# Top-k attention with a maxout MLP: batch 1 in token order too, new ordering offsets, two spans for the last batch

## The chip, the cores and the metric

One Trainium2 chip, one core. The metric is the device time of one execution in microseconds. PE is the matmul engine (PEld its weight loads), DVE, ACT and POOL the vector, scalar and GpSimd engines, SP the engine that issues the transfers.

## The reference

```python
batch, n_heads, seq, head_dim = (8, 8, 576, 64)
top_k = 32
scores = scale * np.matmul(q, k.transpose(0, 1, 3, 2))
kth = np.partition(scores, -top_k, axis=-1)[..., -top_k:-top_k + 1]
mask = scores >= kth
scores = np.where(mask, scores, -1000000000.0)
scores = scores - np.max(scores, axis=-1, keepdims=True)
attn = np.exp(scores)
attn = attn / (np.sum(attn, axis=-1, keepdims=True) + 1e-09)
attn_out = np.matmul(attn, v)
x = attn_out.transpose(0, 2, 1, 3).reshape(4608, 512)
h = np.maximum(np.maximum(x @ w1, x @ w2), x @ w3)   # 512 x 768 weights
out = h @ w_out                                      # 768 x 512
```

All is float32. So each query row keeps its 32 largest scores of 576, and the attention output goes through an MLP whose hidden layer is the maximum of three products.

## The kernel before, in words

**Attention.** A unit (`units`, L872) is a batch, one head pair and two tiles of 128 query tokens, called (0, 1) and (2, 3); the last 64 tokens of two head pairs make a narrow unit of one tile. Ten units make a batch, eight wide and two narrow. For a unit, PE makes the scores (`qk`, L514), ACT moves them to SBUF (`evac`, L523), DVE takes the eight largest of each of 8 groups (`sweep`, L532) and works a pivot out of them, ACT and POOL take the scores on one side of the pivot (L571, L576), DVE finds the threshold among them (L580) and masks the scores (`mask`, L619), ACT exponentiates (`expo`, L628), PE transposes (L679), ACT moves the result (L687), PE multiplies with v (`values`, L704), and DVE, ACT and POOL write the result x as a high and a low float16 part (L721, L724, L728). Before a head pair is used its q and k are loaded by SP (`load_qk`), transposed by PE (L454, L465), scaled by ACT (L460, L469), rounded by ACT (L470) and their rest taken by POOL (L474): one preparation (`prep`, `prepare`). Only two head pairs' preparations are held at a time, six tiles of v, and x for two batches. The scale of v is common to the batch, so that the first values of a batch need all four of its v tiles.

**MLP.** `mlp` (L735) works on spans of tokens of a batch: 0 to 256 as soon as all heads have written these tokens, then 256 to 576. For a span and each of 6 blocks of the hidden layer, three products of 12 matmuls each (`layer`, L760; float16 high and low parts), whose maximum is taken by ACT and DVE (L767, L769) and split by ACT and POOL (L772, L775). Then the output matmuls for each tile of 128 tokens (`layer2`, L820), a scaled copy by ACT (L825) and a store by SP. For the last batch the second span is cut in two, 256 to 512 and 512 to 576 (L1056). A span has 6 x 3 x 12 = 216 matmuls of L760, whatever its width.

**Order.** Nothing of the order on an engine is left to the compiler. Each operation is a `Piece` with an engine, a planned cost, the pieces that it needs, and the buffers that it takes (`Ring`). `in_order` (L65) plans the run, piece by piece, and issues each engine's instructions in that order. A piece's rank is the place of its unit, counted in tiles, plus an offset of its kind from `OFFSETS` (L38; the key `s00` is the first sweep, `m0` the first mask, `Pl` to `Pz` the preparation, `D` and `C` the weights). For each engine the pieces are tried in order of rank, those no more than `LEAD` above the lowest rank that is left; the first that can start within `PATIENCE` (ns) of the earliest is taken. The MLP's pieces stand in a queue of their own (`fill`): on PE one of them goes ahead when it can start more than `AHEAD_OF_FILL` ns before the attention piece; on the other engines they are tried first. DVE pieces marked `alone`, the masks among them, are planned apart from POOL's work. The weights are loaded, decoded on DVE and cut into parts in the first part of the run.

**Batch 0** (`SPLIT`, L133; `batch`, L859) is worked in token order: first the units (0, 1) of all head pairs, in the order 2, 3, 0, 1, then all the rest, head pairs 0 and 1 and then 2 and 3. As only two preparations are held, those of head pairs 2 and 3 are made twice. The other batches go by head pairs: (0, 1) and (2, 3) of pair 0, (0, 1) of pair 1, the narrow unit, (2, 3) of pair 1, and then the same with pairs 2 and 3. In the last batch the second group is sorted so that (0, 1) of both come first and the narrow unit last. The program has 34 preparations.

After the last batch a flag is formed from the numbers that `review` keeps; a second path, for inputs where the threshold was not found, is not taken here.

Of the kernel before, what the change touches and what calls it, by code (L numbers as in the profile page):

```python
# [28 lines left out]
GAP = 100.0  # L29
NEAR = 110.0  # L30
SWITCH = 95.0
AHEAD_OF_FILL = 3
WINDOW = 150
LEAD = 43.3
SLACK = 2000.0
LOCK_A = -150.0
LOCK_B = -100.0
OFFSETS = {'C0': -8.46, 'C1': -18.47, 'C2': 3.93, 'C3': 15.97, 'D0': -3.87, 'D1': -3.6, 'D2': -21.98, 'D3': 12.25, 'E00': 3.88, 'E01': 0.84, 'E02': -2.21, 'E10': -0.98, 'E11': -2.42, 'E12': -13.91, 'N': 0.27, 'Pa': -3.56, 'Pl': -8.36, 'Pp': 14.6, 'Pz': 7.25, 'R': 10.23, 'S': -1.09, 'T00': -15.17, 'T01': -13.99, 'T02': 4.17, 'T10': -11.04, 'T11': -8.12, 'T12': 22.63, 'U': -1.67, 'U0': 2.18, 'V': -13.7, 'V0': -0.21, 'Y': 0.84, 'Z': -6.48, 'd0': 7.84, 'd1': -2.02, 'e00': -1.82, 'e01': -1.45, 'e10': -1.05, 'e11': 1.55, 'g0': 1.61, 'g1': -2.4, 'g2': 1.3, 'g3': -10.18, 'h0': 2.46, 'h1': -2.33, 'h2': 1.34, 'k0': 0.45, 'k1': -2.6, 'k2': 2.19, 'k3': -8.03, 'm0': -18.11, 'm1': -7.69, 'm2': -3.59, 'm3': -1.01, 'p1': 3.73, 'p2': 4.11, 'p3': -13.92, 'p4': -15.96, 'p5': 2.73, 'q0': -0.76, 'q1': -0.22, 'r0': 1.77, 'r1': -17.21, 's00': 5.74, 's01': 5.23, 's10': 5.37, 's11': 6.45, 'v': 13.6, 'w0': 9.7, 'w1': 11.03, 'w2': 0.57, 'w3': 18.45, 'x0': 3.87, 'x1': 2.76, 'x2': 8.01, 'x3': 5.15, 'y': -13.4, 'z0': 3.01, 'z1': 4.39}  # L38
AHEAD = 4
LATE = {'PE': 102.0, 'DVE': 60.0, 'ACT': 95.0, 'POOL': 10.0, 'SP': 2000.0}  # L40

# [88 lines left out]


WS_ACT = range(12)
SPLIT = (0,)  # L133
FIRST = ((0, 1),)
NSM = 2
PATIENCE = {'PE': 2.0, 'DVE': 159.0, 'ACT': 47.0, 'POOL': 7.0, 'SP': 0.0}


@with_exitstack
def kernel(ctx, tc, q, k, v, moe_w1, moe_w2, moe_w3, moe_w_out, out):  # L140
    nc = tc.nc
    B, H, S, D = q.shape
    P = 128
    C = S // 64
    NP = H // 2
    NU = S // P
# [167 lines left out]
    def piece(engine, cost, run, needs=(), rank=(0.0, None), takes=(), mode=None, alone=False):  # L314
        x = Piece(engine, cost, run, needs, rank, [(rings[r], rel) for r, rel in takes], mode, alone)
        pieces.append(x)
        return x
# [102 lines left out]
    def load_qk(b, hp):  # L420
        tiles = []
        for src, nm in ((q, "qt"), (k, "kt")):
            t = io.tile([P, NU, 2, D], F32, name=nm, bufs=1)
            for h in range(2):
                nc.sync.dma_start(t[:, :, h, :], main_rows(src, b, 2 * hp + h))
            tiles.append(t)
        t = io.tile([P, 2, D], F32, name="last", bufs=1)
        for w, src in enumerate((k, q)):
            nc.sync.dma_start(t[64 * w:64 * w + 64], src[at.get(b, b), 2 * hp:2 * hp + 2, MAIN:S].rearrange("h p d -> p h d"))
        tiles.append(t)  # L430
        qk_of[b, hp] = tiles
# [303 lines left out]
    def mlp(b, first, spans, tiles, alone, needs, rank):  # L735
# [4 lines left out]
        products, every, done = [], [], {}  # L740

        def add(engine, cost, run, needs=(), takes=(), mode=None):
            x = Piece(engine, cost, run, needs, rank, [(rings[r], rel) for r, rel in takes], mode)
            every.append(x)
            if engine == "PE":
                if products:
                    x.needs.append(products[-1])
                products.append(x)
            return x

        def layer(i, f, kcs, c0, c1, box):
            if first and not H:
                H.extend(wk.tile([P, FC, HW], F16, name=nm, bufs=1) for nm in ("hh", "hl"))
            xh, xl = x_of[b]
            if kcs[0] == 0:
                box["ps", i] = ps_m.tile([P, 512], F32, name="m")
            for kc in kcs:
                high, low = halves(i, kc, f * P, P)
                for k, (a, bb) in enumerate(((high, xh), (low, xh), (high, xl))):
                    nc.tensor.matmul(box["ps", i][:, :c1 - c0], a, bb[:, kc, c0:c1], start=(kc == 0 and k == 0),  # L760
                                     stop=(kc == KC - 1 and k == 2))
# [15 lines left out]
        for c0, c1 in spans:  # L777
            w = c1 - c0
            base = c0 if c0 < MAIN else c0 - 2 * P
            cs = slice(off + c0 - base, off + c1 - base)  # L780
            for f in range(FC):
                box, prev, before = {}, None, []
                for i in range(3):
                    rel = []
                    for kcs in ((0, 1), (2, 3)):
                        x = add("PE", 6 * max(0.423 * w, 64.0), lambda i=i, f=f, kcs=kcs, c0=c0, c1=c1, box=box: layer(i, f, kcs, c0, c1, box),
                                [*needs, *(lows[i * KC + kc, f * P // CUT * CUT] for kc in kcs if lows)],
                                [("m", rel)] if kcs[0] == 0 else [])
                    now = []
                    y = add("DVE" if i else "ACT", 117 + 1.047 * w if i else 152 + 0.844 * w, lambda i=i, w=w, box=box: largest(i, w, box),  # L790
                            [x, *prev] if i else [x], [("h1", now)])
                    rel.append(y)
                    if i:
                        before.append(y)
                    before, prev = now, [y]
                y = add("ACT", 87 + 0.85 * w, lambda f=f, cs=cs, w=w, box=box: high_h(f, cs, w, box), prev)
                z = add("POOL", 150 + 1.906 * w, lambda f=f, cs=cs, w=w, box=box: low_h(f, cs, w, box), [y])
                before.extend([y, z])
                done.setdefault(f, []).append(z)
        last = products[-1]  # L800
# [36 lines left out]
        for u in tiles:  # L837
# [3 lines left out]
            n = P if u < NU or both else 64  # L841
            at0 = off + u * P - base
            cs = slice(at0, at0 + n)
            box, rel, used = {}, [], []
            for f in range(FC):
                x = add("PE", 3 * 215.0, lambda f=f, cs=cs, n=n, box=box: layer2(f, cs, n, box),
                        [*done[f], *(z for k, z in lows.items() if k[0] == 3 * KC + f)], [("m", rel)] if f == 0 else [])
            y = add("ACT", 585, lambda n=n, both=both, box=box: scaled_out(n, both, box), [x, so_at[b]], [("ob", used)])
# [24 lines left out]
    n = len(units)  # L873
    place_of = [sum(len(x[2]) for x in units[:i]) for i in range(n)]

    preps, starts, prep_of = [], [], []
# [7 lines left out]
    def attention(n):  # L884

        b, hps, us = units[n]
# [51 lines left out]
        for g in gs:  # L938
# [7 lines left out]
            for i in range(3):  # L946
                rel = []
# [8 lines left out]
        rel, takes = [], []  # L956
# [39 lines left out]
    load_last, users = [], [[] for _ in preps]  # L996

    def prepare(pi):
        b, hp = preps[pi]
        rank = starts[pi]  # L1000
        load = piece("SP", 4000, lambda: load_qk(b, hp), list(load_last), (rank, "Pl"))
        box = {}
        load_last.clear()
        done, last = [], list(load_bits)
        load_bits.clear()
        for k in range(3):
            def products(k=k):
                if k == 0:
                    box["turns"] = prep(b, hp)
                box["turns"][k][0]()  # L1010
            rel = []
            x = piece("PE", 109 if k == 0 else 436, products, [load, *done[-1:]], (rank, "Pp"), [("tr", rel)])
            y = piece("ACT", 169 if k == 0 else 1211, lambda k=k: box["turns"][k][1](), [x, *last, *done[-1:]], (rank, "Pa"))
            rel.append(y)
            load_last.append(x)
            if pi >= 2:
                users[pi - 2].append(x)
            done.append(y)
            if k:
                z = piece("POOL", 1380, lambda k=k: box["turns"][k][2](), [y], (rank, "Pz"))  # L1020
                done.append(z)
                load_bits.append(z)
        prepared[pi] = done
# [29 lines left out]
    parts_of = {b: [(True, [(0, 2 * P)], (0, 1)), (False, [(2 * P, S)], range(2, NU + 1))] for b in range(B)}  # L1053
    if len(FIRST) > 1:
        parts_of[0] = [(True, [(0, P)], (0,)), (False, [(P, 2 * P)], (1,)), (False, [(2 * P, S)], range(2, NU + 1))]
    parts_of[B - 1] = [(True, [(0, 2 * P)], (0, 1)), (False, [(2 * P, 4 * P)], (2, 3)), (False, [(4 * P, S)], (NU,))]  # L1056
    for b in range(B):
        for first, spans, tiles in parts_of[b]:
            us = [u for u in range(NU + 1) if any(c0 < u * P + 64 <= c1 or c0 < (u + 1) * P <= c1 for c0, c1 in spans)]
            needs = [z for (hp, u), z in z_of[b].items() if u in us]  # L1060
            products, every, last = mlp(b, first, spans, tiles, False, needs, (0.0, None))
# [89 lines left out]
```

## Time and profile before

| what | us |
|---|---|
| median of 3 runs | 1276.28 (1276.07 to 1277.53) |
| the profiled execution | 1279.52 |
| its span, first to last instruction | 1277.8 |
| PE, DVE, ACT, POOL busy | 1165.9, 1157.3, 1118.2, 684.9 |

The span lies inside the execution's own time; 1.7 us are around it. Busy time is the time in which at least one instruction of the engine ran. Matmuls are pipelined and their ends are modelled, so a PE that is busy all the time isn't thereby at its peak. PEclk is the mean share of full speed that TensorE's clock was granted in a stretch.

### The profile page before, as it was taken

The numbers are of one execution on the slowest core, as the hardware profiler recorded it, in microseconds if no ns is written. First come the engines' busy times: TensorE is split into PE (matmuls) and PEld (weight loads), VectorE is DVE, ScalarE is ACT, GpSimd is POOL, SyncE is SP. The second block draws the span as 40 slices with busy tenths as digits, with TensorE's granted clock in tenths as the row PEclk, the third lists the DMA queues.
The fourth block names the chain that finished last, engine by engine and source line by source line (L and its number), as shares of the span: only waits on it lengthen the run. The fifth ranks groups of instructions, "written<-read, shape, count | busy, mean of one in ns | idle before, by whom it ended". The sixth has DMA issues, their size and how long they took to land.

```text
span 1277.8 us, 30699 instructions
## 1 busy us (share of the span) xinstructions
PE 1165.9 (91%) x9949; PEld 855.3 (67%) x9949; DVE 1157.3 (91%) x5736; ACT 1118.2 (88%) x2912; POOL 684.9 (54%) x625
## 2 busy tenths in 40 slices
PE   4337897999799999999999999999999999999997
PEld 3224574766487766867686766867787777867775
DVE  6999999999999999999999999999999999999221
ACT  5699989999999999999999999999999999998321
POOL 4538477664565565655465565555556555545110
PEclk9667899899799999999999999999999999999999
DMA  7341110211011012110111011010111100000000
GB/s 223 129 117 45 51 38 17 49 38 46 20 39 41 25 29 54 30 36 25 51 38 37 20 37 47 20 53 22 46 30 46 30 21 26 20 18 2 17 18 28
DMA packets 107018, 53.58 MB, mean 42 GB/s; under 512 B 91745, under 2 KB 99937, under 8 KB 106849
## 3 DMA queue, kind: packets, MB, share of 16 engines
q1 hardware_dynamic: 106848, 51.54, 14.7%
q8 instruction: 80, 1.31, 0.4%
q14 instruction: 90, 0.73, 0.2%
HBM read 42.07 MB, written 9.44 MB: 40 GB/s over the span
## 4 chain that ended last, share of the span: by engine, by line
PE 33%; DVE 26%; ACT 20%; POOL 4%; issue 2%; SPq 0%; DMA 0%; ACTq 0%; DVEq 0%; POOLq 0%
PE m L760 16%; DVE L L532 6%; DVE ssb L619 6%; DVE Q L580 4%; ACT w L571 4%; PE m L820 4%; ACT pm L628 4%; PE tr L704 4%; ACT pT L687 4%; PE tr L679 4%; POOL w L576 3%; PE s L514 3%; ACT ssb L523 3%; DVE h L769 2%; DVE nR L556 1%
## 5 line engine op out<-in xcount | busy, mean ns | idle before, releaser
L576 POOL TENSOR_TENSOR w<-ssb,w 128x576 f32<-128x576 f32 x288 | 413.6, 1454 | 135.2 <-ACT w L571 134.3
L760 PE MATMUL m<-xh,wall 128*128 128x256 f16 (+2 forms) x2448 | 436.9, 279 | 1.3 <-DVE h L769 0.6
L760 PEld LDWEIGHTS <-wall 128*128 128x128 f16 x3672 | 343.8, 98 | 79.7 <-issue 7.4
L760 PE MATMUL m<-xl,wall 128*128 128x256 f16 (+2 forms) x1224 | 335.2, 279 | 0.0
L532 DVE MAX8 L<-ssb 128x8 f32<-128x72 f32 x2304 | 329.7, 219 | 2.2 <-ACT ssb L523 2.2
L619 DVE SCALAR_TENSOR_TENSOR ssb<-ssb,kth 128x576 f32<-128x576 f32 x288 | 240.8, 864 | 2.3
L628 ACT ACTIVATE pm<-ssb,nb 128x576 f32<-128x576 f32 x288 | 225.5, 785 | 18.5 <-DVE ssb L619 18.3
L571 ACT ACTIVATE w<-ssb,Q 128x576 f32<-128x576 f32 x288 | 226.1, 786 | 6.8 <-DVE Q L563 6.8
L687 ACT COPY pT<-tr 128x512 f32<-128x512 f32 (+1 forms) x432 | 217.8, 520 | 11.3 <-PE tr L676 7.9
L580 DVE MAX8 Q<-w 128x8 f32<-128x576 f32 x288 | 213.9, 750 | 9.7 <-POOL w L576 8.3
L679 PE MATMUL tr<-ident,pm 128*128 128x128 f32 x1152 | 183.3, 285 | 28.4 <-ACT pm L628 13.2
L514 PE MATMUL s<-kT,qT 64*128 64x288 f32 x1920 | 179.8, 322 | 23.0 <-ACT ssb L523 14.7
L523 ACT COPY ssb<-s 128x576 f32<-128x576 f32 x288 | 185.0, 646 | 4.2 <-PE s L514 3.8
L679 PEld LDWEIGHTS tr<-ident,pm 128*128 128x128 f32 x1152 | 130.8, 143 | 80.2 <-ACT pm L628 27.3
L704 PE MATMUL tr<-pT,vt 128*64 128x256 f32 (+1 forms) x1920 | 180.9, 340 | 2.3 <-ACT pT L687 2.1
L514 PEld LDWEIGHTS s<-kT,qT 64*128 64x128 f32 x1920 | 140.6, 195 | 62.0 <-issue 23.8
L775 POOL TENSOR_TENSOR hl<-h,hh 128x256 f16<-128x256 f32 (+2 forms) x102 | 78.3, 768 | 180.2 <-ACT hh L772 171.1
L769 DVE SCALAR_TENSOR_TENSOR h<-m,rises,h 128x256 f32<-128x256 f32 (+2 forms) x204 | 100.4, 492 | 60.1 <-PE m L760 55.9
L704 PEld LDWEIGHTS tr<-pT,vt 128*64 128x64 f32 x1920 | 109.5, 141 | 60.9 <-issue 15.8
L820 PE MATMUL m<-wall,hh 128*128 128x512 f16 x432 | 128.9, 379 | 3.6 <-POOL wall L305 1.9
L728 POOL TENSOR_TENSOR xl<-xs,xh 128x256 f16<-128x256 f32 (+1 forms) x80 | 52.4, 655 | 126.6 <-ACT xh L724 126.6
L474 POOL TENSOR_TENSOR kT<-raws,kT 128x576 fp32r<-128x576 f32 x34 | 49.7, 1462 | 86.2 <-ACT kT L470 83.8
(109 smaller groups left out, 1468.2 us busy)
## 6 DMA issues: line engine op xcount, KB each, us to landing
wall<-in_moe_w_dram SPq DMA_DIRECT2D x12, 768.0 KB, 5.9
qt<-in_q_dram SPq DMA_DIRECT2D x68, 128.0 KB, 2.9
kt<-in_k_dram SPq DMA_DIRECT2D x68, 128.0 KB, 3.0
out_dram<-ob SPq DMA_DIRECT2D x32, 256.0 KB, 2.3
vt<-in_v_dram SPq DMA_DIRECT2D x32, 128.0 KB, 2.1
vt<-in_v_dram SPq DMA_DIRECT2D x32, 64.0 KB, 2.2
vt<-in_v_dram SPq DMA_DIRECT2D x96, 16.0 KB, 2.0
vt<-in_v_dram SPq DMA_DIRECT2D x32, 48.0 KB, 2.2
```

The costliest lines, as they stand in the source:

```text
L514: nc.tensor.matmul(s[:, h, :HALF], qT[sl, qa, c0:c0 + P], kT[sl, ka, i * HALF:(i + 1) * HALF], start=(n_ == 0), stop=(n_ == len(runs) - 1))
L523: nc.scalar.copy(d["both", g][:, :, i * HALF:(i + 1) * HALF], d["s"].pop((g, i))[:, :, :HALF])
L532: nc.vector.max(d["L"][:, t, k, :], d["ssb"][t][:, k * GW:(k + 1) * GW])
L571: nc.scalar.activation(d["w"][t], d["ssb"][t], AF.Sign, bias=d["Q"][:, t, 0:1], scale=-1.0, accum_out=d["cnt"][:, t:t + 1])
L576: nc.gpsimd.tensor_tensor(d["w"][t], d["ssb"][t], d["w"][t], ALU.mult)
L580: nc.vector.max(d["Q"][:, t, 1:NW], d["w"].pop(t))
L619: nc.vector.scalar_tensor_tensor(ss, ss, d["kth"][:, t:t + 1], ss, ALU.is_lt, ALU.subtract, accum_out=d["lost"][:, t:t + 1])
L628: nc.scalar.activation(d["pm", t // 2][:, t % 2], d["ssb"][t], AF.Exp, bias=d["nb"][:, t:t + 1], scale=-1.0 / SHRINK, accum_out=d["sums"][ ...
L679: nc.tensor.transpose(pt[:, j * P:(j + 1) * P], pm[:, i, 64 * i + j * P:64 * i + (j + 1) * P], ident)
L687: nc.scalar.copy(pT[:, 512 * i:512 * i + m] if i < 2 else pT[:, 8 * P:10 * P], pt[:, :m])
L704: nc.tensor.matmul(to, vt[:, block if i < 4 else 8 + h, :], keys, start=(i == 0), stop=(i == 4))
L760: nc.tensor.matmul(box["ps", i][:, :c1 - c0], a, bb[:, kc, c0:c1], start=(kc == 0 and k == 0), stop=(kc == KC - 1 and k == 2))
```

## The change

Batch 1 joins batch 0 in `SPLIT`, so its units go in token order too; its head pairs 2 and 3 are then prepared twice, and the program has 36 preparations. The line that cut the last batch's MLP in three spans goes, so that it has two like the others. The pieces of batch 0's units and preparations get keys of their own, with an underscore in front, in `OFFSETS`; all offsets have new values. `LEAD`, `PATIENCE` and `AHEAD_OF_FILL` have new values, and the planned cost of an MLP matmul is changed: 0.9 ns more for wide ones, and a lower floor for narrow ones. No instruction of a unit or of the MLP changes in kind.

```diff
-AHEAD_OF_FILL = 3
+AHEAD_OF_FILL = 21
-LEAD = 43.3
+LEAD = 73.4
-OFFSETS = {'C0': -8.46, 'C1': -18.47, 'C2': 3.93, 'C3': 15.97, 'D0': -3.87, 'D1': -3.6, 'D2': -21.98,
...
+OFFSETS = {'C0': -24.16, 'C1': -8.19, 'C2': 8.62, 'C3': 19.5, 'D0': -5.71, 'D1': -5.65, 'D2': -49.21,
...
+ '_Pa': -2.68, '_Pl': -11.11, '_Pp': -3.76, '_Pz': -17.42, '_T00': -32.25, '_T01': -13.55, '_T02': 7.86,
...
-SPLIT = (0,)
+SPLIT = (0, 1)
-PATIENCE = {'PE': 2.0, 'DVE': 159.0, 'ACT': 47.0, 'POOL': 7.0, 'SP': 0.0}
+PATIENCE = {'PE': 27.0, 'DVE': 197.0, 'ACT': 65.0, 'POOL': 109.0, 'SP': 0.0}
...
-                        x = add("PE", 6 * max(0.423 * w, 64.0), lambda ...
+                        x = add("PE", 6 * max(0.423 * w + 0.9, 29.0), lambda ...
...
-        p = lambda key, *a, **kw: ... rank=(place_of[n], key ...
+        p = lambda key, *a, **kw: ... rank=(place_of[n], ("_" if b == 0 else "") + (key ...
...
-        rank = starts[pi]
-        load = piece("SP", 4000, lambda: load_qk(b, hp), list(load_last), (rank, "Pl"))
+        rank, first_ = starts[pi], "" if b else "_"
+        load = piece("SP", 4000, lambda: load_qk(b, hp), list(load_last), (rank, first_ + "Pl"))
...
     parts_of = {b: [(True, [(0, 2 * P)], (0, 1)), (False, [(2 * P, S)], range(2, NU + 1))] for b in range(B)}
...
-    parts_of[B - 1] = [(True, [(0, 2 * P)], (0, 1)), (False, [(2 * P, 4 * P)], (2, 3)), (False, [(4 * P, S)], (NU,))]
```

## Rows read from the trace of the kernel before

**Rows 1.** The page's first part: busy time, share of the span, instructions.

```profile
PE 1165.9 (91%) x9949; PEld 855.3 (67%) x9949; DVE 1157.3 (91%) x5736; ACT 1118.2 (88%) x2912; POOL 684.9 (54%) x625
```

**Rows 2.** Stretches by stage: length, busy of each engine, PEclk, DMA share, GB/s.

```profile
0.00:148.00 148.00, 75.80 (x412) 49.50 (x413) 133.79 (x520) 115.44 (x284) 78.40 (x89) 0.75 0.40 122
148.00:240.00 92.00, 79.17 (x706) 58.91 (x704) 87.33 (x433) 82.26 (x216) 61.39 (x65) 0.96 0.13 32
...
240.00:378.00 138.00, 126.82 (x1078) 91.97 (x1078) 134.45 (x698) 132.07 (x348) 80.72 (x66) 0.95 0.14 36
...
317.00:352.00 35.00, 25.93 (x187) 17.25 (x184) 32.88 (x189) 33.48 (x88) 18.98 (x15) 0.80 0.10 25
...
378.00:514.00 136.00, 133.39 (x1147) 97.38 (x1146) 131.37 (x669) 128.66 (x339) 74.42 (x64) 1.00 0.14 37
514.00:658.00 144.00, 143.86 (x1278) 108.56 (x1276) 141.27 (x754) 137.79 (x360) 81.31 (x71) 1.00 0.13 34
658.00:796.00 138.00, 134.19 (x1151) 96.68 (x1149) 136.46 (x696) 131.60 (x350) 82.68 (x68) 1.00 0.15 37
796.00:932.00 136.00, 135.42 (x1192) 100.30 (x1190) 131.65 (x696) 130.92 (x345) 73.06 (x65) 1.00 0.13 35
932.00:1064.00 132.00, 131.79 (x1162) 98.52 (x1160) 127.38 (x667) 127.86 (x337) 76.46 (x65) 1.00 0.12 30
...
1193.00:1278.00 85.00, 77.38 (x750) 59.34 (x748) 16.07 (x42) 17.49 (x42) 10.07 (x19) 0.98 0.06 21
```

(In each row: PE, PEld, DVE, ACT, POOL busy us with the number of instructions.)

**Rows 3.** Timeline: last low part of x that a first half needs; its first matmul.

```profile
351.48 0.67 POOL L728 TENSOR_TENSOR xl<-xs,xh 128x256 f16<-128x256 f32 x1
352.29 0.38 PE L760 MATMUL m<-xh,wall 128*128 128x256 f16 x2
...
489.65 0.67 POOL L728 TENSOR_TENSOR xl<-xs,xh 128x256 f16<-128x256 f32 x1
499.69 0.38 PE L760 MATMUL m<-xh,wall 128*128 128x256 f16 x2
...
630.40 0.67 POOL L728 TENSOR_TENSOR xl<-xs,xh 128x256 f16<-128x256 f32 x1
633.29 0.38 PE L760 MATMUL m<-xh,wall 128*128 128x256 f16 x2
...
1162.49 0.67 POOL L728 TENSOR_TENSOR xl<-xs,xh 128x256 f16<-128x256 f32 x1 [1.05 <-ACT xh L724]
...
1195.08 0.38 PE L760 MATMUL m<-xh,wall 128*128 128x256 f16 x2
```

**Rows 4.** Timeline: the last batch's third span, its first matmul, and what follows it.

```profile
1257.89 0.22 PE L760 MATMUL m<-xh,wall 128*128 128x64 f16 x2
...
1266.93 0.59 PE L820 MATMUL m<-wall,hh 128*128 128x512 f16 x2
```

**Rows 5.** The chain that ended last: start, us, what; 320 and then 256 columns.

```profile
568.79 4.89 PE m L760 x36
...
1226.71 23.58 PE m L760 x216
```

**Rows 6.** Groups by line and shape, preparations: count, busy us, mean ns, idle before.

```profile
L474 POOL TENSOR_TENSOR qT<-raws,qT 128x576 fp32r<-128x576 f32 x34 | 50.8, 1493 | 29.6 <-ACT qT L470 29.5
...
L469 ACT ACTIVATE raws<-tr 128x512 f32<-128x512 f32 x68 | 41.5, 610 | 1.4 <-PE tr L465 1.4
L465 PE MATMUL tr<-ident,qt 128*128 128x128 f32 x136 | 22.9, 295 | 2.8 <-ACT pT L687 1.8 <-ACT raws L469 0.9
L470 ACT CAST qT<-raws 128x576 fp32r<-128x576 f32 x34 | 22.9, 673 | 1.1
...
L460 ACT ACTIVATE raws<-tr 128x128 f32<-128x128 f32 x34 | 10.1, 298 | 8.0 <-PE tr L454 8.0
```

**Rows 7.** Timeline of DVE: masks without and with a POOL instruction beside.

```profile
1175.36 0.81 DVE L619 SCALAR_TENSOR_TENSOR ssb<-ssb,kth 128x576 f32<-128x576 f32 x1
...
1176.61 1.44 DVE L619 SCALAR_TENSOR_TENSOR ssb<-ssb,kth 128x576 f32<-128x576 f32 x1
```

More of the change, by code (lines that the diff above doesn't have):

```diff
@@ L37 @@
 LOCK_B = -100.0
-OFFSETS = {'C0': -8.46, 'C1': -18.47, 'C2': 3.93, 'C3': 15.97, 'D0': -3.87, 'D1': -3.6, 'D2': -21.98, 'D3': 12.25, 'E00': 3.88, 'E01': 0.84, 'E02': -2.21, 'E10': -0.98, 'E11': -2.42, 'E12': -13.91, 'N': 0.27, 'Pa': -3.56, 'Pl': -8.36, 'Pp': 14.6, 'Pz': 7.25, 'R': 10.23, 'S': -1.09, 'T00': -15.17, 'T01': -13.99, 'T02': 4.17, 'T10': -11.04, 'T11': -8.12, 'T12': 22.63, 'U': -1.67, 'U0': 2.18, 'V': -13.7, 'V0': -0.21, 'Y': 0.84, 'Z': -6.48, 'd0': 7.84, 'd1': -2.02, 'e00': -1.82, 'e01': -1.45, 'e10': -1.05, 'e11': 1.55, 'g0': 1.61, 'g1': -2.4, 'g2': 1.3, 'g3': -10.18, 'h0': 2.46, 'h1': -2.33, 'h2': 1.34, 'k0': 0.45, 'k1': -2.6, 'k2': 2.19, 'k3': -8.03, 'm0': -18.11, 'm1': -7.69, 'm2': -3.59, 'm3': -1.01, 'p1': 3.73, 'p2': 4.11, 'p3': -13.92, 'p4': -15.96, 'p5': 2.73, 'q0': -0.76, 'q1': -0.22, 'r0': 1.77, 'r1': -17.21, 's00': 5.74, 's01': 5.23, 's10': 5.37, 's11': 6.45, 'v': 13.6, 'w0': 9.7, 'w1': 11.03, 'w2': 0.57, 'w3': 18.45, 'x0': 3.87, 'x1': 2.76, 'x2': 8.01, 'x3': 5.15, 'y': -13.4, 'z0': 3.01, 'z1': 4.39}
+OFFSETS = {'C0': -24.16, 'C1': -8.19, 'C2': 8.62, 'C3': 19.5, 'D0': -5.71, 'D1': -5.65, 'D2': -49.21, 'D3': 13.66, 'E00': 4.97, 'E01': -2.15, 'E02': -3.62, 'E10': -2.81, 'E11': -8.06, 'E12': -7.96, 'N': 1.32, 'Pa': -3.57, 'Pl': 0.52, 'Pp': 4.31, 'Pz': 2.8, 'R': 10.83, 'S': -0.82, 'T00': -18.98, 'T01': -13.16, 'T02': 2.46, 'T10': -24.66, 'T11': -7.29, 'T12': 13.64, 'U': -0.57, 'U0': 1.15, 'V': -12.5, 'V0': 0.59, 'Y': -1.08, 'Z': -17.03, '_E00': 3.11, '_E01': 4.71, '_E02': -10.42, '_E10': -6.66, '_E11': 3.37, '_E12': -36.82, '_N': 2.29, '_Pa': -2.68, '_Pl': -11.11, '_Pp': -3.76, '_Pz': -17.42, '_T00': -32.25, '_T01': -13.55, '_T02': 7.86, '_T10': -13.39, '_T11': -0.01, '_T12': 7.91, '_Y': -3.57, '_Z': -12.72, '_d0': 7.09, '_d1': -36.76, '_e00': -14.0, '_e01': -0.34, '_e10': -8.78, '_e11': 2.09, '_g0': 1.93, '_g1': -5.5, '_g2': 3.41, '_g3': 2.15, '_h0': 0.08, '_h1': 3.92, '_h2': 0.1, '_k0': -2.63, '_k1': -5.49, '_k2': 5.69, '_k3': -7.12, '_m0': -22.4, '_m1': -8.74, '_m2': -8.4, '_m3': -2.08, '_p1': 2.89, '_p2': 5.28, '_p3': -13.82, '_p4': -14.42, '_p5': 2.96, '_q0': -5.3, '_q1': -4.63, '_r0': 5.43, '_r1': -19.16, '_s00': 5.29, '_s01': 2.26, '_s10': 5.97, '_s11': 4.01, '_v': 24.49, '_w0': 5.3, '_w1': 4.17, '_w2': 10.22, '_w3': 18.02, '_x0': -0.87, '_x1': -1.09, '_x2': 8.04, '_x3': 4.86, '_y': -12.58, '_z0': 0.67, '_z1': 4.44, 'd0': 10.55, 'd1': -5.38, 'e00': -1.77, 'e01': 1.78, 'e10': 3.3, 'e11': 0.88, 'g0': 2.05, 'g1': 0.16, 'g2': 2.06, 'g3': -1.97, 'h0': 2.43, 'h1': -9.03, 'h2': 5.73, 'k0': -8.7, 'k1': 5.12, 'k2': 5.95, 'k3': -7.69, 'm0': -16.37, 'm1': -8.3, 'm2': 1.16, 'm3': 4.23, 'p1': 4.37, 'p2': 5.05, 'p3': -14.28, 'p4': -18.22, 'p5': 4.77, 'q0': -6.74, 'q1': -4.74, 'r0': 2.62, 'r1': -15.28, 's00': 5.97, 's01': 4.31, 's10': 5.39, 's11': 4.99, 'v': 7.41, 'w0': -0.21, 'w1': 7.37, 'w2': -15.87, 'w3': 11.31, 'x0': 7.69, 'x1': -0.36, 'x2': 10.99, 'x3': 5.7, 'y': -14.4, 'z0': 3.95, 'z1': -7.09}
@@ L785, in mlp @@
                     for kcs in ((0, 1), (2, 3)):
-                        x = add("PE", 6 * max(0.423 * w, 64.0), lambda i=i, f=f, kcs=kcs, c0=c0, c1=c1, box=box: layer(i, f, kcs, c0, c1, box),
+                        x = add("PE", 6 * max(0.423 * w + 0.9, 29.0), lambda i=i, f=f, kcs=kcs, c0=c0, c1=c1, box=box: layer(i, f, kcs, c0, c1, box),
                                 [*needs, *(lows[i * KC + kc, f * P // CUT * CUT] for kc in kcs if lows)],
@@ L890, in attention @@
         d = of[n] = {}
-        p = lambda key, *a, **kw: d.setdefault(key, piece(*a, rank=(place_of[n], key if isinstance(key, str) else "".join(map(str, key))), **kw))
+        p = lambda key, *a, **kw: d.setdefault(key, piece(*a, rank=(place_of[n], ("_" if b == 0 else "") + (key if isinstance(key, str) else "".join(map(str, key)))), **kw))
         needs, takes = [z for k in prep_of[n] for z in prepared[k]], []
@@ L1011, in prepare @@
             rel = []
-            x = piece("PE", 109 if k == 0 else 436, products, [load, *done[-1:]], (rank, "Pp"), [("tr", rel)])
-            y = piece("ACT", 169 if k == 0 else 1211, lambda k=k: box["turns"][k][1](), [x, *last, *done[-1:]], (rank, "Pa"))
+            x = piece("PE", 109 if k == 0 else 436, products, [load, *done[-1:]], (rank, first_ + "Pp"), [("tr", rel)])
+            y = piece("ACT", 169 if k == 0 else 1211, lambda k=k: box["turns"][k][1](), [x, *last, *done[-1:]], (rank, first_ + "Pa"))
             rel.append(y)
@@ L1019, in prepare @@
             if k:
-                z = piece("POOL", 1380, lambda k=k: box["turns"][k][2](), [y], (rank, "Pz"))
+                z = piece("POOL", 1380, lambda k=k: box["turns"][k][2](), [y], (rank, first_ + "Pz"))
                 done.append(z)
```

## The prediction, made before the changed kernel ran

> **What bounds the kernel now.** I read the page first. PE and DVE are both busy 91% of the span and ACT 88% [rows 1], so no single engine can be named from the averages, and a stage table is needed. I cut the span where a batch's last attention result is written (240, 378, 514, 658, 796, 932, 1064, 1193 us) and added three cuts for the MLP's first halves [rows 2]. The reader is to see three regimes. Up to 148 us PE works half the time (75.8 of 148) at a mean granted clock of 0.75, because no MLP work exists yet. From 240 to 1163 us DVE is busy all but some 1 to 4% and PE all but some 3% of nearly every stage; the one hole is 317 to 352 us, where PE is busy 25.93 of 35 us and the granted clock is 0.80, between its levels of 1.2 and 2.4 GHz. From 1193 us on DVE has nothing but MLP crumbs (16.07 of 85) and PE runs the last batch's MLP alone.
>
> Then I asked whether the MLP waits for attention or for PE. The MLP of a batch's first 256 tokens can start when POOL has written the low part of the last head pair's x (L728), and does start with its first L760 matmul. The paired rows give both times [rows 3]. Batch 1: ready at 352.15 (351.48 + 0.67), started at 352.29, so PE had been starved. Batch 2: ready 490.32, started 499.69, 9.4 us late. Batch 3: ready 631.07, started 633.29, 2.2 us late. Batch 7: ready 1163.16, started 1195.08, 32 us late. So PE runs behind from batch 2 on, but by little until late; then the backlog grows, and the end is a PE queue with its last 77.38 busy us after attention is over [rows 2].
>
> **The change, part by part.**
>
> *Two spans for the last batch.* The 64-token span disappears; its columns join the 256-token span ahead of it. It runs from 1257.89 to 1266.93, 9.04 us [rows 4]. The chain's rows give 23.58/216 = 0.1092 us per 256-column matmul and 4.89/36 = 0.1358 us per 320-column one [rows 5]; the 216 matmuls grow by 216 x 0.0266 = 5.7 us. Saved: 3.3 us of PE where PE alone sets the end. The output matmuls stay the same in number. DVE, ACT and POOL save some short instructions, beside PE, worth nothing. **-3.3**.
>
> *Batch 1 in token order.* The MLP's first half then needs four wide units of batch 1, not seven and a narrow one. Nine such widths of attention fill the 138 us of that batch [rows 2], 15 us each, so four units and a unit's latency end about 240 + 4 x 15 + 10 = 310 us (an estimate), ahead of 317, where the fill ran out. The hole closes; at most its 9.1 idle us of PE come free [rows 2]. They do not reach the end by themselves: started 35 us earlier, batch 1's MLP would end near 465 us and wait for batch 2's first half, ready at 490; and the slack at that boundary is 9.4 us, at the next 2.2 [rows 3]. What is late next is attention, which DVE sets. So I carry the smallest slack, **-2.2**, between 0 and -9.1. V tiles: batch 1's first-loaded tiles are now held until the batch ends, so batch 2's third and fourth V loads and its value scale come late, as batch 1's do now; DVE's idle in 240 to 378, 3.55 us of 138 [rows 2], is all that this boundary costs today, and I add nothing. If that cover went, batch 2's first value matmuls would queue behind it on PE.
>
> *Two more preparations.* The heads 2 and 3 of batch 1 are loaded and transposed twice. Each costs ACT 2 x 0.610 + 2 x 0.673 + 0.298 = 2.86 us, so 5.7 in all, and POOL 4 x 1.493 = 6.0 [rows 6]. They fall into 240 to 378 us, where ACT is busy 132.07 of 138 us and POOL 80.72 [rows 2]: 5.9 us of ACT are free, just enough. PE's 18 transposes, at 0.295 us [rows 6] at most 5.3 us if none overlapped, go into the hole's 9.1 idle us. SP issues 12 more transfers and starts them ahead of the V loads; the stage's DMA share is 0.14 and no engine's wait in it ends with a transfer, so that queue costs nothing while it stays so short. Behind a late ACT piece stand the evacuations of scores, and behind these DVE. POOL may also slow DVE: a mask instruction takes 0.81 us alone and 1.44 beside POOL work [rows 7], so four more POOL instructions cost DVE at most 4 x 0.63 = 2.5 us. The Trainium skill (GPSIMD Engine Reference, Specifications) says that POOL shares its SBUF interfaces with VectorE and names two-input VectorE instructions as those that contend, which these rows bear out; by that rule alone all four would collide and the term would stand at its full 2.5. The planner keeps masks away from POOL for most of the run, so I stay near the lower end: between 0 and 5.7 + 2.5 = 8.2 I take **+2**, because the row of ACT's free time, 5.9, nearly covers the work.
>
> *New offsets, patience, lead and fill margin.* These change no instruction, only the order on each engine; the matmul cost edit (0.9 ns a matmul at 256 columns) only shifts planned times and is worth nothing itself. No row shows the new order. The batches take 138, 136, 144, 138, 136, 132 and 129 us [rows 2]; the excess of the longer three over the median 136 is 2 + 8 + 2 = 12 us. I take half of it, **-6**. One bound is a gain of half of DVE's idle before 932 us: 14.2 + 4.7 + 3.5 + 4.6 + 2.7 + 1.5 + 4.4 = 35.6, so -18. The other is one more batch as slow as the third, +8. Batch 0's own offsets belong here: its 240 us hold the 14.2 and 4.7. Where a long batch is shortened, what is late next is PE, which already lags.
>
> *Sum.* -3.3 - 2.2 + 2 - 6 = -9.5. The profiled execution took 1279.5 us with a span of 1277.8; less 9.5 that is 1270.0. It lies 3.2 us above the median 1276.3 of the runs shown, so I forecast 1266.8 there.
>
> **Rivals.**
>
> *ACT becomes batch 1's bound (slower).* If the 5.7 us of preparation do not fit into ACT's 5.9 idle us, which are scattered behind its own waits, and POOL adds its 2.5 on DVE, batch 1 ends 8.2 us later and every later batch with it; this decides once the delay passes the 2.2 us of slack at batch 3. With the merge and no gain from the order: 1276.3 + 8.2 - 3.3 = 1281.2. For it speaks ACT's 96% in that stage; against it that batch 0 is split already and its boundary costs DVE little.
>
> *Nothing moves (same).* The early MLP work only waits at 490 us, the order gains nothing, the merge pays for the preparations: 1276.3 - 3.3 + 2 = 1275.0. The weight loads take 97.38 of 136 and 98.52 of 132 us, 72 and 75% [rows 2], so PE may have room that its busy time hides; then neither the hole nor the backlog counts. The Trainium skill (Perfetto Trace Analysis, Identifying the Most-Contended Engine) states that rule: judge PE by weight loads, not by matmul time. Against it speak the 32 us by which ready work starts late at batch 7.
>
> *The order pays in full (much faster).* Half of DVE's idle before 932 us goes, and the slack of 2.2 and the merge with it, at no cost for the preparations: 1276.3 - 18 - 2.2 - 3.3 = 1252.8. For it speaks that the last two full batches already take 132 and 129 us; against it that DVE and PE are both within 3% of full, so one cannot be moved without the other.
>
> The change does do what it says: batch 1 becomes split by the one tuple, and batch 0's keys get their underscore where pieces are ranked; only weights and batch-end pieces keep shared keys.
>
> **How the numbers follow.** About 0.2% (2.6 us) is what a measurement of this kernel can tell from no change. The forecast case has 0.50, ACT's rival 0.18, nothing 0.16, the full gain 0.16. Faster is the first and last together, 0.66; same 0.16; slower 0.18. The forecast's own range is 1258 to 1273. The range that should hold 8 in 10 reaches to the full gain's value, 1253, and to 1281, about the price of the slow rival, leaving about half of each outside.
>
> **What would show it.** Right: no 64-column L760; 36 low parts of kT; L760 matmuls from about 310 us without a break to 352 and a granted clock near 1.0 there; batch 1's preparations inside ACT's gaps, its end at 378 or earlier; first halves of later batches started with no more delay than now; the last attention result near 1185. Wrong: ACT above 98% in batch 1 with DVE waiting on score evacuations, a batch above 144 us, or a new hole of PE ahead of 490 us that comes back as a longer tail. The forecast falls if attention ends no earlier than 1193 and the tail behind it stays at 85 less 3.3 us.

## The result and the profile after

The changed kernel takes 1284.85 us (median of 6 runs, 1284.35 to 1286.37) against 1277.62 us (6 runs) for the kernel before: a ratio of 1.0060, 95% interval 1.0049 to 1.0072. It is 7 us slower. The forecast was 1266.8, and the time lies outside its range as well, beyond the slow rival's 1281.2. The profiled execution took 1285.65 us, its span is 1283.8.

The page of the changed kernel, first part, answers to [rows 1]:

```profile
PE 1178.1 (92%) x9751; PEld 855.7 (67%) x9751; DVE 1152.7 (90%) x5724; ACT 1120.9 (87%) x2910; POOL 692.3 (54%) x623
```

DVE is busy 4.6 us less than before and the span is 6 us longer, so the loss is no added work on DVE, the engine by which the prediction paced attention; it is idle time. The stretches by stage answer to [rows 2] (length, then busy us of PE, PEld, DVE, ACT, POOL, PEclk, DMA share, GB/s):

```profile
0.00:148.00 148.00, 76.07 (x389) 48.94 (x390) 130.32 (x495) 112.78 (x275) 75.46 (x88) 0.69 0.39 118
148.00:240.00 92.00, 78.68 (x663) 58.64 (x661) 83.11 (x419) 78.73 (x203) 64.59 (x64) 0.90 0.16 42
240.00:261.00 21.00, 15.85 (x85) 10.62 (x86) 17.35 (x61) 18.94 (x48) 11.17 (x8) 0.55 0.16 38
...
317.00:352.00 35.00, 34.58 (x318) 25.00 (x316) 32.38 (x174) 34.49 (x93) 20.81 (x17) 1.00 0.12 34
...
514.00:658.00 144.00, 142.69 (x1255) 106.11 (x1255) 141.24 (x733) 138.04 (x363) 81.66 (x71) 1.00 0.13 34
658.00:796.00 138.00, 136.76 (x1178) 99.91 (x1175) 135.81 (x712) 131.46 (x344) 79.16 (x67) 1.00 0.14 37
```

The hole at 317 to 352 us is gone, as forecast: PE 34.58 busy of 35 us at a clock of 1.00, against 25.93 at 0.80 [rows 2]. But a stage ahead of it got worse. Up to 240 us DVE is busy 130.32 + 83.11 = 213.4 us, against 133.8 + 87.3 = 221.1 before, and from 240 to 261 us it idles another 3.7 us; TensorE's granted clock is 0.55 there. The last result of batch 0 is written at 260.75 us (the first line below, 260.01 + 0.74), not at 240.

The pairs of readiness and start answer to [rows 3] (batch 0's second span, then the first halves of batches 1, 2 and 7):

```profile
260.01 0.74 POOL L728 TENSOR_TENSOR xl<-xs,xh 128x256 f16<-128x256 f32 x1 [6.96 <-ACT xh L724]
261.37 0.43 PE L760 MATMUL m<-xh,wall 128*128 128x320 f16 x2
...
319.20 0.67 POOL L728 TENSOR_TENSOR xl<-xs,xh 128x256 f16<-128x256 f32 x1 [2.85 <-ACT xh L724]
339.84 0.38 PE L760 MATMUL m<-xh,wall 128*128 128x256 f16 x2
...
490.17 0.38 PE L820 MATMUL m<-wall,hl 128*128 128x512 f16 x1
502.68 0.68 POOL L728 TENSOR_TENSOR xl<-xs,xh 128x256 f16<-128x256 f32 x1 [0.26 <-ACT xh L724]
503.05 0.38 PE L760 MATMUL m<-xh,wall 128*128 128x256 f16 x2
...
1176.28 0.68 POOL L728 TENSOR_TENSOR xl<-xs,xh 128x256 f16<-128x256 f32 x1
1203.98 0.38 PE L760 MATMUL m<-xh,wall 128*128 128x256 f16 x2
```

Batch 1's first half is ready at 320 us and starts at 339.84, 12 us earlier than before: up to there PE is still at batch 0's second span, which started 21 us later than before (261.37 against 240.17). So up to 340 us the old hole is filled by work that is late, which the forecast did not mean, and only from there on by batch 1. The MLP of batch 1 is done at 490.6, and then the fill runs dry for 12.5 us, until batch 2's first half comes at 503. Batch 2 starts 3.4 us later than before, batch 7 8.9 us later.

Batch by batch, from the end of the last L728 of one to that of the next (us):

| batch | 0 | 1 | 2 | 3 | 4 | 5 | 6 | 7 |
|---|---|---|---|---|---|---|---|---|
| before | 239.5 | 139.0 | 135.4 | 143.8 | 138.0 | 136.4 | 132.0 | 129.2 |
| changed | 260.7 | 131.1 | 134.1 | 138.3 | 138.7 | 137.5 | 131.9 | 126.4 |

Batch 0 takes 21.2 us longer, and the others give 15.6 back, 13.4 of them in batches 1 and 3. Attention ends 5.6 us later (the last result, before and changed):

```profile
1192.78 0.43 POOL L728 TENSOR_TENSOR xl<-xs,xh 128x128 f16<-128x128 f32 x1 [4.30 <-ACT xh L724]
```

```profile
1198.33 0.43 POOL L728 TENSOR_TENSOR xl<-xs,xh 128x128 f16<-128x128 f32 x1 [1.85 <-ACT xh L724]
```

The end of the chain answers to [rows 4, 5] (start, us, what):

```profile
1204.14 23.58 PE m L760 x216
1227.72 7.77 PE m L820 x36
1235.49 29.34 PE m L760 x216
1264.83 11.67 PE m L820 x54
1276.50 0.03 ACTq L825
```

From batch 7's first MLP matmul to the last output matmul it is 1276.50 - 1203.98 = 72.5 us, against 1270.99 - 1195.08 = 75.9 before: the merge gave its 3.4 us. So the span's 6.0 us are 8.9 lost before 1204 less 3.4 gained behind, and 0.5 at the end.

### The profile page after: what moved, and what is told of

Same layout as the page of the kernel before. It is cut to its first block, busy times and chain, and to the rows that moved or that the text cites. A ratio compares the mean times of both kernels' runs of the same rounds, so it can differ in the third digit from the quotient of the medians.

```text
span 1283.8 us, 30311 instructions
## 1 busy us (share of the span) xinstructions
PE 1178.1 (92%) x9751; PEld 855.7 (67%) x9751; DVE 1152.7 (90%) x5724; ACT 1120.9 (87%) x2910; POOL 692.3 (54%) x623
## 5 line engine op out<-in xcount | busy, mean ns | idle before, releaser
L760 PE MATMUL m<-xh,wall 128*128 128x256 f16 (+1 forms) x2304 | 434.6, 286 | 0.4 <-ACT h L767 0.4
L760 PEld LDWEIGHTS <-wall 128*128 128x128 f16 x3456 | 336.7, 98 | 81.8 <-issue 5.6
L760 PE MATMUL m<-xl,wall 128*128 128x320 f16 (+1 forms) x1152 | 329.2, 286 | 0.0
L619 DVE SCALAR_TENSOR_TENSOR ssb<-ssb,kth 128x576 f32<-128x576 f32 x288 | 238.9, 858 | 2.2
L679 PE MATMUL tr<-ident,pm 128*128 128x128 f32 x1152 | 183.1, 287 | 24.4 <-ACT pm L628 13.4
L514 PE MATMUL s<-kT,qT 64*128 64x288 f32 x1920 | 182.1, 325 | 22.3 <-ACT ssb L523 14.3
L704 PE MATMUL tr<-pT,vt 128*64 128x256 f32 (+1 forms) x1920 | 186.2, 345 | 4.0 <-ACT pT L687 2.3
L523 ACT COPY ssb<-s 128x576 f32<-128x576 f32 x288 | 184.6, 644 | 3.6 <-PE s L514 3.1
L769 DVE SCALAR_TENSOR_TENSOR h<-m,rises,h 128x256 f32<-128x256 f32 (+1 forms) x192 | 97.4, 507 | 53.5 <-PE m L760 50.2
L775 POOL TENSOR_TENSOR hl<-h,hh 128x256 f16<-128x256 f32 (+1 forms) x96 | 77.0, 802 | 125.0 <-ACT hh L772 124.6
L820 PE MATMUL m<-wall,hh 128*128 128x512 f16 x432 | 129.2, 380 | 0.2 <-POOL wall L305 0.2
L728 POOL TENSOR_TENSOR xl<-xs,xh 128x256 f16<-128x256 f32 (+1 forms) x80 | 54.0, 676 | 109.9 <-ACT xh L724 109.9
L474 POOL TENSOR_TENSOR kT<-raws,kT 128x576 fp32r<-128x576 f32 x36 | 52.3, 1454 | 80.7 <-ACT kT L470 79.3
```

Of the source, the lines that this page charges most:

```text
L514: nc.tensor.matmul(s[:, h, :HALF], qT[sl, qa, c0:c0 + P], kT[sl, ka, i * HALF:(i + 1) * HALF], start=(n_ == 0), stop=(n_ == len(runs) - 1))
L523: nc.scalar.copy(d["both", g][:, :, i * HALF:(i + 1) * HALF], d["s"].pop((g, i))[:, :, :HALF])
L619: nc.vector.scalar_tensor_tensor(ss, ss, d["kth"][:, t:t + 1], ss, ALU.is_lt, ALU.subtract, accum_out=d["lost"][:, t:t + 1])
L679: nc.tensor.transpose(pt[:, j * P:(j + 1) * P], pm[:, i, 64 * i + j * P:64 * i + (j + 1) * P], ident)
L704: nc.tensor.matmul(to, vt[:, block if i < 4 else 8 + h, :], keys, start=(i == 0), stop=(i == 4))
```

## The experiments

The prediction held that the planned cost of an MLP matmul is worth nothing and that the order would gain. Two theories stood at first: that the split costs (S), or that the new numbers, offsets and planner's limits, cost (O). After e4 a third, F, was put against S: the offsets fit one exact set of planned times, and every edit of a planned time or of the list of work throws the order out of fit. Ratios are to the kernel before, run on the same chip beside each experiment.

**e1: two last spans alone**, on the kernel before.

```diff
-    parts_of[B - 1] = [(True, [(0, 2 * P)], (0, 1)), (False, [(2 * P, 4 * P)], (2, 3)), (False, [(4 * P, S)], (NU,))]
```

> The kernel before with the last batch's MLP in two spans and nothing else. Both theories: the 64-token span goes, worth 3.3 us of PE in the tail, so a ratio of 0.9974 and about 1274.3 us; the last attention result stays at 1193 us. If the plan of the whole run shifts with the shorter list, attention's end may move by some us either way.

Measured 1275.03 us, ratio 0.9983 (0.9973 to 0.9993). The merge is right in sign and near in size: 2.2 us, 0.9 to 3.4 by the interval.

**e2: the split alone**, on the kernel before.

```diff
-SPLIT = (0,)
+SPLIT = (0, 1)
```

> The kernel before with batch 1 in token order and nothing else (old offsets, three last spans). Theory S (the split itself costs: two preparations, and the MLP runs dry again ahead of batch 2): 6 to 9 us slower, 1284 to 1287. Theory O (the new offsets and planner numbers cost, the split is about even): within 3 us of before, 1275 to 1281.

Measured 1293.32 us, 1.0118 (1.0100 to 1.0137): 15 us slower, more than either theory said. Much of it is DVE's own time: the masks are 288 as before, but take 250.2 us in all instead of 240.8 (the group in the page's listing: busy us, mean ns, idle before).

```profile
L619 DVE SCALAR_TENSOR_TENSOR ssb<-ssb,kth 128x576 f32<-128x576 f32 x288 | 250.2, 896 | 2.1
```

The MLP's hole moved as well. From 453 to 505 us this kernel runs 3 matmuls of L760 (the first row; PE, PEld, PEclk, DMA share, GB/s); batch 1's output matmuls go on until 479.05, and from there to 504.86, 25.8 us, PE has no MLP work:

```profile
453.00:505.00 52.00, 0.22 (x3) 0.23 (x3) 0.90 0.18 45
...
478.67 0.38 PE L820 MATMUL m<-wall,hl 128*128 128x512 f16 x1
...
504.86 0.38 PE L760 MATMUL m<-xh,wall 128*128 128x256 f16 x2
```

So the work that became ready early was done early, and PE then waited for batch 2.

**e3: the changed kernel without the split** (`SPLIT = (0,)`).

> The changed kernel with batch 1 by head pairs again, all else kept. Theory S: the 9 us come back, 1274 to 1278 us. Theory O: no faster than the changed kernel, 1283 to 1290, and batch 0 still ends near 260 us instead of 240.

Measured 1303.56 us, 1.0207 (1.0190 to 1.0224). Neither theory had this: the split costs with the old numbers, and taking it away costs with the new ones. Batch 0 ends at 249.2 us, so theory O's 260 was a miss as well. The effects don't add; the numbers belong to the list of work.

**e4: the changed kernel with three last spans** (the deleted line put back).

> The changed kernel with the last batch's MLP in three spans again. Both theories: 3.3 us slower than the changed kernel, about 1288 us, batch 0's end unmoved at 261 us.

Measured 1287.72 us, 1.0081 (1.0064 to 1.0097), as expected within the interval. PE's order is that of the changed kernel up to the last batch's second span. The third span stands at the end of all queues, so it is the one part here that could be added up.

**e5: the changed kernel with the old planned cost.** Its instructions are the same in kind and number; the order is the same until some 9 us behind the first MLP matmul (at 151.9 us in the changed kernel), on DVE until 160 us and on PE until 168 us, and differs from there on.

```diff
-                        x = add("PE", 6 * max(0.423 * w + 0.9, 29.0), lambda ...
+                        x = add("PE", 6 * max(0.423 * w, 64.0), lambda ...
```

> The changed kernel with the planned cost of an MLP matmul as it was (0.423 ns a column, without the 0.9 ns); offsets, split and two spans stay. The instructions are the same, only the planned order differs. Theory F (the offsets fit one exact set of planned costs; the 0.9 ns throw the plan out of fit): 10 to 14 us come back, 1271 to 1275, and batch 0 ends near 245 instead of 261 us. Theory S (the split costs, the cost edit is worth nothing): 1283 to 1287.

Measured 1278.29 us, 1.0002 (0.9990 to 1.0014). The changed kernel's 0.6% are gone, so this one line carries them, although it is a bit less than theory F said (1271 to 1275): with the old cost the rest of the change is worth nothing on balance. Stretches of the changed kernel and of e5, up to where they part and behind (as in rows 2; 0.00:148.00 of the changed kernel stands above, and DVE's idle there is 17.7 us in it and 18.0 in e5):

```profile
148.00:260.00 112.00, 93.53 (x739) 68.43 (x739) 99.46 (x477) 96.67 (x249) 75.02 (x71) 0.83 0.16 41
```

```profile
148.00:260.00 112.00, 97.04 (x817) 71.17 (x813) 108.19 (x523) 101.87 (x267) 75.91 (x73) 0.94 0.18 45
```

DVE idles 12.5 us in the changed kernel and 3.8 in e5: 8.7 us, more than the whole difference. Batch 0 ends at 249.5 us in e5 (the rows below: its last low part, its second span's first matmul), 11.2 us earlier than in the changed kernel; batch 7's MLP starts at 1197.65, 6.3 us earlier, and the span is 6.3 us shorter.

```profile
248.84 0.67 POOL L728 TENSOR_TENSOR xl<-xs,xh 128x256 f16<-128x256 f32 x1
...
248.19 0.43 PE L760 MATMUL m<-xh,wall 128*128 128x320 f16 x2
```

Finer slices show the place, the changed kernel first, then e5:

```profile
212.00:228.00 16.00, 14.34 (x95) 9.01 (x95) 11.77 (x68) 14.92 (x38) 8.59 (x8) 0.93 0.25 71
228.00:244.00 16.00, 10.53 (x78) 8.41 (x80) 14.99 (x78) 12.29 (x31) 10.55 (x8) 0.50 0.23 55
244.00:260.00 16.00, 12.33 (x66) 7.60 (x66) 12.46 (x48) 13.94 (x38) 8.92 (x6) 0.54 0.20 48
```

```profile
212.00:228.00 16.00, 11.98 (x75) 7.96 (x75) 15.41 (x77) 15.73 (x42) 13.25 (x14) 0.79 0.17 37
228.00:244.00 16.00, 14.67 (x124) 9.80 (x124) 15.37 (x66) 14.76 (x39) 8.96 (x7) 0.89 0.34 90
244.00:260.00 16.00, 13.95 (x114) 9.68 (x109) 15.59 (x85) 15.61 (x42) 8.58 (x8) 1.00 0.31 75
```

In the changed kernel the last output matmuls of batch 0's first half end at 222.9 us, and PE has no MLP work for 38 us; in e5 they end at 240.8 and the pause is 7 us. From 212 to 228 us PE spends 6.02 us on output matmuls (L820) in the changed kernel and 1.18 in e5 (the rows of L820 alone: PE, PEld, PEclk, DMA share, GB/s):

```profile
212.00:228.00 16.00, 6.02 (x21) 2.20 (x21) 0.93 0.25 71
```

```profile
212.00:228.00 16.00, 1.18 (x3) 0.28 (x3) 0.79 0.17 37
```

Behind them, with attention's work alone, the clock of the changed kernel is granted at 0.50 and 0.54. And DVE stands in its fixed order behind value products that are late (timeline of DVE, changed kernel; the bracket is the idle time before it and what ended it):

```profile
216.44 0.18 DVE L563 TENSOR_REDUCE Q<-z 128x4 f32<-128x32 f32 x1
220.09 0.48 DVE L721 SCALAR_TENSOR_TENSOR xs<-tr,down_v,pT 128x256 f32<-128x256 f32 x1 [3.47 <-PE tr L704]
220.50 0.63 DVE L532 MAX8 L<-ssb 128x8 f32<-128x72 f32 x4
```

The sweep at 220.50 stands behind that wait; output matmuls run on PE until 217.6, and only then the value products. Two such waits make 6.0 us in 148 to 260. The second, 2.51 us up to 259.01, ends with 20 value products that take 4.50 us, at a clock of 0.54 from 244 to 260; the 20 ahead of the first wait, from 217.60, took 2.38.

**e6: the kernel before with the new planned cost**, e5's edit the other way round.

> The kernel before with the new planned cost of an MLP matmul (0.423 ns a column plus 0.9, lower floor) and nothing else. Theory F: out of fit, 5 to 15 us slower, 1282 to 1292, DVE idle and mask time up. Theory S: an edit of a planned time by under 1% changes nothing, 1275 to 1279.

Measured 1300.68 us, 1.0174 (1.0152 to 1.0196): 22 us for 0.9 ns in a planned time, more than theory F said. (The lower floor touches the 64-column span alone, which comes last in PE's order.) Theory S falls. The stage at fault is in part the same (148 to 260 us, this kernel):

```profile
148.00:260.00 112.00, 95.58 (x779) 69.49 (x778) 103.23 (x494) 94.05 (x246) 66.02 (x68) 0.89 0.12 30
```

DVE idles 8.8 us there, against 4.8 before in the same stretch. The rest is spread: the masks take 245.7 us, and batch 7's MLP starts at 1215.88, 21 us later.

**e7: two spans and the split, old numbers.**

> The kernel before with two last spans and batch 1 in token order, old offsets and costs: the two parts of the change without the new numbers. If the parts add (1.2% for the split alone, -0.2% for two spans alone): 1288 to 1292. Against e5 it shows what the new numbers are worth to the split.

Measured 1288.42 us, 1.0084 (1.0062 to 1.0107), 1.0% over e1. As expected. Against e5's 1.0002, the new numbers are worth 0.8% to the split.

**e8: e5 without the split.**

> As e5 with batch 1 by head pairs again. Theory F: the numbers are fitted to the split too, so taking it away costs, 8 to 20 us over e5. Theory S: taking the split away helps, 5 to 10 us under e5.

Measured 1293.70 us, 1.0118 (1.0101 to 1.0135), 15 us over e5: as theory F said. The new numbers behave as if fitted to the split and to the old cost; how they were found is not known.

**e9: the changed kernel refitted.** Its planned cost keeps the 0.9 ns. 138 of the 144 offsets, most by a few units, and the limits were moved by random steps; a step was kept where the planner's own end came earlier, with room for small steps back.

```diff
-LEAD = 73.4
+LEAD = 89.7
-AHEAD_OF_FILL = 21
+AHEAD_OF_FILL = 10
...
-PATIENCE = {'PE': 27.0, 'DVE': 197.0, 'ACT': 65.0, 'POOL': 109.0, 'SP': 0.0}
+PATIENCE = {'PE': 11.0, 'DVE': 197.0, 'ACT': 62.0, 'POOL': 127.0, 'SP': 0.0}
```

> The changed kernel, its planned matmul cost with the 0.9 ns included, with offsets, lead, patience and fill margin moved by small random steps of which those were kept that ended the plan earlier. Theory F (out of fit with that cost): the loss comes back, 1275 to 1280, with batch 0 ending near 250 us. If the 0.9 ns or the split cost by themselves: it stays at 1283 to 1287.

Measured 1279.41 us, 1.0014 (1.0004 to 1.0023): three quarters of the loss come back with the same list of work and the same planned cost, and batch 0 ends at 252.7 us. So neither the 0.9 ns nor the split costs by itself; what costs is the order that came of them with the unfitted numbers.

**e10: a control, the kernel before with the planned cost 0.6 ns lower.**

```diff
-                        x = add("PE", 6 * max(0.423 * w, 64.0), lambda ...
+                        x = add("PE", 6 * max(0.423 * w - 0.6, 64.0), lambda ...
```

> The kernel before with the planned cost of an MLP matmul 0.6 ns lower (0.423 ns a column less 0.6) and nothing else: a control for e6. Theory F in its plain form (any edit of a planned time that moves the order costs): 5 to 22 us slower, 1282 to 1300. If only a higher planned cost hurts (the plan then gives PE's MLP work too much room): within 3 us of before.

Measured 1301.72 us, 1.0196 (1.0179 to 1.0213), just over theory F's range. The direction didn't matter here. The masks take 12.0 us more than before, about half of the loss:

```profile
L619 DVE SCALAR_TENSOR_TENSOR ssb<-ssb,kth 128x576 f32<-128x576 f32 x288 | 252.8, 903 | 2.2
```

**e11: e1 refitted** in the same way as e9.

> The kernel before with two last spans, its numbers moved by the same small random steps (the plan's end moves by under 0.1%), so another order of the same quality by the plan. If the plan's end tells the chip's time: as e1, 1272 to 1277. If an order that the numbers were not measured with on a chip costs whatever the plan says: 1280 to 1295.

Measured 1273.66 us, 0.9967 (0.9957 to 0.9978), the fastest, ahead of both kernels of this case, and in the range of the first theory. So another order is not worse for being other. Its masks take 240.2 us. The last attention result and batch 7's first MLP matmul, in e1 and then in e11 (timelines of POOL and PE):

```profile
1193.21 0.43 POOL L728 TENSOR_TENSOR xl<-xs,xh 128x128 f16<-128x128 f32 x1 [4.30 <-ACT xh L724]
1195.52 0.38 PE L760 MATMUL m<-xh,wall 128*128 128x256 f16 x2
```

```profile
1178.27 0.43 POOL L728 TENSOR_TENSOR xl<-xs,xh 128x128 f16<-128x128 f32 x1 [4.16 <-ACT xh L724]
1191.73 0.38 PE L760 MATMUL m<-xh,wall 128*128 128x256 f16 x2
```

Attention ends 14.9 us earlier, the last batch's first 256 tokens are ready 14.6 us earlier (1149.0 against 1163.6), and its MLP starts 3.8 us earlier: the rest is PE's queue.

| kernel | list of work | planned cost | numbers | ratio |
|---|---|---|---|---|
| e1 | two spans | old | old | 0.9983 |
| e11 | two spans | old | refitted | 0.9967 |
| e5 | two spans, split | old | new | 1.0002 |
| e9 | two spans, split | new | refitted | 1.0014 |
| changed | two spans, split | new | new | 1.0060 |
| e4 | three spans, split | new | new | 1.0081 |
| e7 | two spans, split | old | old | 1.0084 |
| e8 | two spans | old | new | 1.0118 |
| e3 | two spans | new | new | 1.0207 |
| e2 | three spans, split | old | old | 1.0118 |
| e6 | three spans | new | old | 1.0174 |
| e10 | three spans | lower | old | 1.0196 |

## Why the prediction was wrong

**The step that failed** stands in the part on offsets, patience, lead and fill margin: "the matmul cost edit (0.9 ns a matmul at 256 columns) only shifts planned times and is worth nothing itself". It carries the whole loss against the kernel before: with it undone (e5) the ratio goes from 1.0060 to 1.0002, 7.4 us, and on the kernel before it costs 1.7% by itself (e6). The forecast missed by some 17 us, from -9.5 to +7; the other 9.5 are the rest of its sum, of which e5 shows nothing left. The planner takes, at each step, the piece that it thinks can start first, within a patience of some ns. A group of six matmuls that is planned 5.4 ns longer can turn a near tie, and then all choices behind it. I had costed the edit by its size in planned time; its size is that of the reordering.

**The order's -6** was half right in its mechanism: the long batches 1 and 3 did get shorter, by 7.9 and 5.5 us. What it had wrong is batch 0, whose idle time it counted as something to gain, and which lost 21.2; the term's worst case, +8, was one slow batch in the middle. Nor is there one price of the new numbers: with the split they are worth 0.8% (e7 to e5), without it they cost 1.4% (e1 to e8). Even with the old cost, split and new numbers together cost 0.2% over the two spans alone (e5 against e1), some 2.4 us, with intervals that just overlap.

**The merge's -3.3** was right: 2.2 us in e1, 3.4 between rows of the two kernels' tails.

**The prediction's own test** went against it: the forecast falls "if attention ends no earlier than 1193 and the tail behind it stays at 85 less 3.3 us". Attention ended at 1198.8 and the tail was 85.0 us, so even the merge's gain went, into a last MLP that started 5.2 us after attention's end and not 1.9.

**The split's -2.2** was right in its mechanism: with the split PE goes from batch 0's second span to batch 1's first half without a break (at 329.4 us in e5, 339.8 in the changed kernel, where the late batch 0 helped), and a new hole opened ahead of batch 2, at 490.6 to 503.1, of the kind that the prediction named as a sign of being wrong; it did not come back as a longer MLP at the end. The estimate of readiness, 310 us, was 10 us too early: batch 0 ended 21 us late, and the four units took 59 us and not 70. That the split gains is not borne out. In a list out of fit (e2, e7) it costs 1.0 to 1.2%; orders that fit with it (e5, e9) stand 0.2 to 0.5% over orders that fit without (e1, e11).

**The preparations' +2** were not tried by themselves. ACT's busy time from 240 to 378 us did not rise (132.0 us against 132.07 [rows 2]), since batch 0's end and batch 1 now share the stretch, and the slow rival's place, ACT in batch 1, is not where the time went: batch 1 got 7.9 us shorter, ACT is busy 126.5 of the 131 us from 261 to 392, and DVE's waits for evacuated scores (L523) from 240 to 392 come to 0.4 us.

**The backlog on PE** that the prediction read from [rows 3] is borne out by e11: 14.9 us of attention are worth 3.8 at the start of the last MLP. Behind that start PE alone sets the pace and is busy all the time, and there its weight loads take 50.99 of 72.51 us, 70%:

```profile
1191.73:1264.24 72.51, 72.51 (x523) 50.99 (x521) 13.04 (x28) 14.63 (x29) 8.77 (x12) 1.00 0.05 20
```

So the 72 to 75% that the prediction's rival took for room are what a PE shows here that has none. The Trainium skill (Perfetto Trace Analysis, Identifying the Most-Contended Engine) says to judge TensorE's headroom by how busy the weight loads are; at that end of the run these rows speak against reading it as the distance to 100%.

**Masks beside POOL** [rows 7] were priced for four instructions, 2.5 us at most. They matter for all 288: over the orders tried their sum runs from 238.8 us (e4) to 252.8 (e10). The Trainium skill (GPSIMD Engine Reference, Specifications) says that the two engines share SBUF interfaces, and the traces agree. Counted over them, masks without a POOL tensor operation beside take 0.81 us on the mean in every run; those that start while one is running take 1.17 in the kernel before (35 of them), 1.31 in e10 (46) and 1.17 in e2 (63); and beyond 0.813 us each, these come to 12.6, 23.0 and 22.3 us. Orders out of fit have longer masks in e2, e3, e6, e7 and e10, but not in e8 (240.5); in the changed kernel the masks are short (238.9), so they are not its loss. Why these orders meet POOL more often was not tried.

Left open too: how much of the 0.9 ns edit's effect is chance. Two edits of the cost were tried on the kernel before, and cost 1.7 and 2.0%; one on the changed kernel, back to the old cost, gained 0.6%. Orders might differ by chance alone, and the kernel before be a lucky one; against it speak the two refits, both within 0.4% of it, but two are few. Nor is the plan's own end known for the changed kernel, e6 or e10, and so not whether the planner saw the loss.

## What to carry to other kernels

Where an order is planned greedily from costs and its priorities were fitted, costs, work list and priorities are one object: an edit to any of them is an edit of the whole order, and must be costed as one, or refitted before it is judged. Compare a new list of work with its own refit against the old list with its own refit; otherwise a list is blamed for the numbers (e7) or looks necessary because of them (e3). Here, work that became ready earlier was not worth more than the slack at the boundaries behind it: the hole came back ahead of the next batch.

## What the runs showed that was not expected

A planned time that agrees better with the chip made the order worse: 0.423 x 256 + 0.9 = 109.2 ns is what the rows show (109.2, [rows 5]), the old 108.3 is not, and still the old one gives 1.0002 against 1.0060, and 1.0000 against 1.0174. (For 320 columns the rows' 135.8 lies midway between the old 135.4 and the new 136.3.)

And TensorE's clock differed where the work did not. From 228 to 260 us of the changed kernel, with attention alone, PE was busy 10.53 and 12.33 of 16 us, and the clock was granted at 0.50 and 0.54, at or near its lower level of 1.2 GHz. But up to 148 us the changed kernel and e8 run the same order, and from 50 to 100 us the one was granted 0.57 and the other 1.00:

```profile
50.00:100.00 50.00, 21.51 (x111) 14.57 (x111) 48.30 (x166) 43.07 (x106) 25.78 (x25) 0.57 0.49 144
```

```profile
50.00:100.00 50.00, 22.53 (x111) 15.14 (x111) 48.34 (x165) 42.98 (x106) 25.73 (x25) 1.00 0.50 144
```

It cost next to nothing there: the first MLP matmul starts at 151.90 us in the changed kernel and at 151.72 in e8. Nor is the clock the changed kernel's loss: its six executions had mean clocks of 0.942 to 0.978, and the one at 0.978 took 1284.50 us, no less than the others' 1284.35 to 1286.37.
